# Linear attention and a squared-ReLU feed-forward on one core: batch 0's attention planned with the rest, first loads in order on the SyncE queue

## The chip, the core and the metric

The kernel runs on one core of one Trainium2 chip. The metric is the device time in microseconds (us) of one execution; the kernel before takes 279.13 us (median of 3 runs, 278.8 to 279.6). A profile of one execution comes with it: its span, from the first to the last instruction, is 276.6 us, and that execution took 278.33 us. Names used: PE (TensorE, matmuls), PEld (the loading of PE's weights), DVE (VectorE), ACT (ScalarE), POOL (GpSimd), SP (SyncE, which only issues transfers here). Each engine runs its own instructions in the order in which they were issued, and waits on semaphores for the others.

## What is computed

```python
def phi(x, c, s):                       # c, s: cosine and sine of the position
    r = np.maximum(x, 0.0)
    return np.concatenate([r * c, r * s], axis=-1)
q_p, k_p = phi(q, cos_w, sin_w), phi(k, cos_w, sin_w)      # (8, 8, 576, 128)
kv  = np.einsum('bhsf,bhsd->bhfd', k_p, v)
z   = np.sum(k_p, axis=2)
num = np.einsum('bhsf,bhfd->bhsd', q_p, kv)
den = np.einsum('bhsf,bhf->bhs', q_p, z)[..., None] + 1e-06
x   = (num / den).transpose(0, 2, 1, 3).reshape(4608, 512)
h   = np.maximum(x @ w_in, 0.0)                            # w_in 512 x 2048
out = (h * h) @ w_out                                      # w_out 2048 x 512
```

q, k and v are 8 batches x 8 heads x 576 positions x 64, in float32. There is no softmax: per head a 128 x 64 matrix kv and a vector z are summed over the positions, and every position is then one small product with them. The feed-forward network takes the 4608 rows of x.

## The kernel before, in words

**Tiling.** A batch's 576 positions are four row blocks j = 0 to 3 of 128 positions ("main") and a tail of 64. For each block the cosine and sine features of k and q are made by `relu_scale` (lines 405 and 407, tiles kp and qp), v is cast to bf16 with a column of ones (vx, `copy`, line 412), and PE sums kv and z over the blocks (65 columns per head, tile kvz). q's features are transposed, multiplied by kvz (numerator and denominator), divided on DVE (den, x), and x is transposed to xT. Batch 0 and batch 1 transpose on PE (lines 580 and 668); later batches by transfers (lines 567 and 656). The feed-forward part works on halves of a batch's main rows (256 columns): weights `w1sb` (w_in in bf16, four pieces of 512 columns of w_in, so pieces 0 to 3 hold the blocks 0 to 3, 4 to 7, 8 to 11 and 12 to 15 of 128) times xT, relu on ACT (tile rt or rs), square on DVE (gT), then `w2sb`. Batches 3 to 7 use a Strassen-like scheme of seven products with sums of weights (w1s, made on DVE from w1sb early on) in place of eight; all but batch 0 use it for the second product.

**What sets the order.** From batch 0's third row block on, the order of every engine is the result of `Planner.plan` (line 127 on): a list scheduler with a cost per operation and engine, a place ("slot") for each PE operation from its position, a due time for the others, and pools of buffers. Operations that may run on ACT or DVE are put on one by it. `SHIFTS` is a list of corrections "operation number : shift of its place or due time : engine". Operations of the pseudo-engine GIVEN stand for things that are already under way at a known time, such as the first loads. PE takes the candidate that can start earliest by the planner's times. The order is written into the program, and the semaphores see to the dependences.

**The prologue** (lines 1057 to 1136), the order of which is written by hand: k of batch 0 is issued on SP; kt (k's tail), v, vt, q in two parts, the four w1 pieces, qt and the first w2 piece follow one after another on POOL. 31 matmuls on zeros (line 1069) keep PE busy until k and v have come. Then k's features (cosine on DVE, sine on ACT), v's casts, 40 matmuls into the two banks of kv, the features, transposes and numerators of row blocks 0 and 1 for all 8 heads, a divide per block, seven more matmuls without result (line 1132) and the transposes of x. The planner's clocks start after it (line 1219: PE at 16.8, ACT at 17.3, DVE at 17.1).

**The start of the planned part.** Features of q for row blocks 2 and 3 and the tail, their transposes and numerators, among the feed-forward groups of batch 0 (`declare_plain`, lines 694 to 724). A group is 8 matmuls: 2 blocks of w1 x 4 parts of the contraction, on 256 columns of xT. The groups of the first piece on the first half (`split`) are cut into two of 128 columns, so that they can begin with row block 0 alone. Planning rates of PE are on line 437: 0.1092 us per 256 columns, 0.0586 per 128, 0.0296 per 65, 0.066 per transpose.

```python
    given = lambda keys, t, **kw: add(("GIVEN", 0.0), lambda _: None, w=keys, pos=t, **kw)
    for i in range(4):
        given([("w1", i)], 12.2, size=2.6)
```

**After that** come, on POOL's queue, q, k and v of batches 1 and 2 and the w2 pieces; from batch 3 on the loads are on SP's queue.

## Time and profile before

| engine | busy us | share of the span |
|---|---|---|
| PE | 269.0 | 97% |
| PEld | 227.8 | 82% |
| DVE | 219.1 | 79% |
| ACT | 192.6 | 70% |
| POOL | 28.4 | 10% |

HBM is read for 36.70 MB and written for 9.44 MB, 167 GB/s over the span; the granted clock of PE is at 0.9 or more of full speed in all 40 slices.

How to read it. A row of the timeline gives the start in us, the duration, the engine (POOL's and SP's transfer issues are rows too), the line, the operation, out<-in with shapes, and in brackets the idle time of that engine just before it with what ended it. In a row of several instructions ("x24") the first start and the total time stand. The busy time of PE also counts matmuls that give no result, such as the first 31 (9.76 us from 1.20 us on). A matmul's own row can miss a few records, weight loads (PEld) have one row for every matmul, so counts go by them. In the rows of busy time by stretch, the columns are the stretch, its length, busy time and number of instructions of PE, PEld, DVE, ACT and POOL, the granted clock, the busy share of the transfer engines, and GB/s. For a tile, "to landing" is the time from the start of an issue until the data are there.

### The profile page before, as it was taken

The numbers are of one execution on the slowest core, as the hardware profiler recorded it, in microseconds if no ns is written. First come the engines' busy times: TensorE is split into PE (matmuls) and PEld (weight loads), VectorE is DVE, ScalarE is ACT, GpSimd is POOL, SyncE is SP. The second block draws the span as 40 slices with busy tenths as digits, with TensorE's granted clock in tenths as the row PEclk, the third lists the DMA queues.
The fourth block names the chain that finished last, engine by engine and source line by source line (L and its number), as shares of the span: only waits on it lengthen the run. The fifth ranks groups of instructions, "written<-read, shape, count | busy, mean of one in ns | idle before, by whom it ended". The sixth has DMA issues, their size and how long they took to land.

```text
span 276.6 us, 7125 instructions
## 1 busy us (share of the span) xinstructions
PE 269.0 (97%) x2846; PEld 227.8 (82%) x2851; DVE 219.1 (79%) x515; ACT 192.6 (70%) x385; POOL 28.4 (10%) x46
## 2 busy tenths in 40 slices
PE   8979999999999999999999999999999999999994
PEld 3658856789888988888888888988988888888883
DVE  1849996998795896799977999799946997279741
ACT  3767862798798796499848995699738643685421
POOL 8925244100000000000000000000000000000000
PEclk9999999999999999999999999999999999999999
DMA  7999999776999999899899428997583301200024
GB/s 228 311 206 287 330 256 374 220 174 148 368 191 257 281 248 238 220 331 160 237 266 377 114 40 167 330 219 210 57 233 77 94 32 42 112 1 2 8 88 134
DMA packets 77824, 53.01 MB, mean 192 GB/s; under 512 B 52032, under 2 KB 73024, under 8 KB 77792
## 3 DMA queue, kind: packets, MB, share of 16 engines
q1 hardware_dynamic: 70368, 37.63, 54.7%
q0 software_dynamic: 7280, 14.81, 19.8%
q8 instruction: 22, 0.36, 0.5%
q10 hardware_dynamic: 144, 0.13, 0.1%
q14 instruction: 10, 0.08, 0.1%
HBM read 36.70 MB, written 9.44 MB: 167 GB/s over the span
## 4 chain that ended last, share of the span: by engine, by line
PE 81%; DVE 11%; DMA 2%; issue 2%; POOL 2%; ACT 1%; POOLq 0%; DVEq 0%
PE banks L429 78%; DVE gT L418 3%; DVE rs L421 3%; DVE gs L426 3%; DMA q<-in_q_dram 2%; PE banks L580 1%; DVE gTt L418 1%; PE banks L668 1%; PE banks L1132 1%; ACT qp L405 1%; POOL kt L365 1%; DVE x L628 1%; POOL vt L365 0%; ACT sums L412 0%; DVE kp L407 0%
## 5 line engine op out<-in xcount | busy, mean ns | idle before, releaser
L429 PEld LDWEIGHTS <-w1sb 128*128 128x128 bf16 x784 | 72.7, 98 | 8.7
L429 PE MATMUL banks<-xT,w1sb 128*128 128x256 bf16 (+1 forms) x576 | 68.3, 267 | 0.1
L429 PEld LDWEIGHTS <-gs 128*128 128x128 bf16 x512 | 49.5, 98 | 7.0 <-DVE gs L426 0.7
L429 PE MATMUL banks<-w2sb,gT 128*128 128x256 bf16 (+1 forms) x284 | 44.8, 295 | 0.2 <-issue 0.2
L429 PEld LDWEIGHTS <-gT 128*128 128x128 bf16 x400 | 37.4, 98 | 7.5
L415 ACT ACTIVATE rt<-banks 128x512 bf16<-128x512 f32 x64 | 37.2, 602 | 9.2 <-PE banks L429 4.5
L429 PEld LDWEIGHTS <-w1s 128*128 128x128 bf16 x320 | 30.6, 98 | 3.9 <-issue 0.2
L429 PE MATMUL banks<-w2sb,gs 128*128 128x256 bf16 x256 | 32.7, 273 | 0.1
L429 PE MATMUL banks<-w2s,gs 128*128 128x256 bf16 x256 | 32.1, 273 | 0.1
L421 DVE CUSTOM_DVE_ANT_0 rs<-banks,sums 128x512 bf16<-128x512 f32 x40 | 27.0, 684 | 3.8 <-ACT sums L829 3.1
L418 DVE TENSOR_TENSOR gT<-rs 128x1024 bf16<-128x1024 bf16 (+1 forms) x50 | 28.0, 580 | 1.2 <-ACT rs L415 0.6
L426 DVE TENSOR_TENSOR ysb<-banks,sums 128x256 f32<-128x256 f32 x32 | 13.5, 422 | 17.6 <-PE banks L429 9.4
L418 DVE TENSOR_TENSOR gT<-rt 128x512 bf16<-128x512 bf16 x48 | 19.4, 420 | 7.1 <-ACT rt L415 7.0
L415 ACT ACTIVATE rs<-banks 128x512 bf16<-128x512 f32 x40 | 23.5, 606 | 2.0 <-PE banks L429 1.8
L405 ACT ACTIVATE kp<-k,sin_col 128x512 bf16<-128x512 f32 x32 | 22.4, 725 | 0.5 <-DMA k<-in_k_dram 0.5
L429 PE MATMUL banks<-xT,w1s 128*128 128x256 bf16 x160 | 22.7, 273 | 0.0
L429 PE MATMUL banks<-xs,w1s 128*128 128x256 bf16 x160 | 22.7, 273 | 0.0
L405 ACT ACTIVATE qp<-q,sin_col 128x512 bf16<-128x512 f32 x32 | 22.0, 720 | 1.0 <-DMA q<-in_q_dram 1.0
L426 DVE TENSOR_TENSOR gs<-gT 128x1024 bf16<-128x1024 bf16 x28 | 19.2, 689 | 3.1 <-PE banks L429 2.7
L628 DVE TENSOR_TENSOR x<-banks,den 128x512 bf16<-128x512 f32 x30 | 20.7, 691 | 1.0
L429 PE MATMUL banks<-xTt,w1sb 128*128 128x256 bf16 x128 | 16.1, 273 | 0.0
L407 DVE TENSOR_SCALAR kp<-k,cos_col 128x512 bf16<-128x512 f32 x26 | 12.0, 501 | 5.0 <-DMA k<-in_k_dram 5.0
(105 smaller groups left out, 362.8 us busy)
## 6 DMA issues: line engine op xcount, KB each, us to landing
out_dram<-ysb SPq DMA_DIRECT2D x13, 512.0 KB, 3.6
k<-in_k_dram SPq DMA_DIRECT2D x6, 1024.0 KB, 6.4
v<-in_v_dram SPq DMA_DIRECT2D x5, 1024.0 KB, 7.5
q<-in_q_dram SPq DMA_DIRECT2D x5, 1024.0 KB, 9.3
v<-in_v_dram POOLq DMA_DIRECT2D x3, 1024.0 KB, 8.2
w1sb<-in_moe_w_in_dram POOLq DMA_DIRECT2D x4, 512.0 KB, 10.9
w2sb<-in_moe_w_out_dram POOLq DMA_DIRECT2D x4, 512.0 KB, 12.4
q<-in_q_dram POOLq DMA_DIRECT2D x2, 1024.0 KB, 9.1
```

What stands on the lines that cost most here:

```text
L365: eng.dma_start(out=tail[g * TAIL : (g + 1) * TAIL, :, :], in_=src[b, g * HH : (g + 1) * HH, MAIN:S, :].rearrange("h p d -> p h d"),)
L405: nc.scalar.activation(out=dst, in_=src, func=ACTF.Relu, scale=col)
L407: nc.vector.tensor_scalar(out=dst, in0=src, scalar1=0.0, scalar2=col, op0=ALU.max, op1=ALU.mult)
L415: nc.scalar.activation(out=out, in_=in_, func=ACTF.Relu)
L418: nc.vector.tensor_tensor(out=out, in0=in_, in1=in_, op=ALU.mult)
L421: nc.vector._custom_dve(TENSOR_ADD_SAT, out=out, in0=in0, in1=in1, s0=float("inf"), s1=0.0)
L426: nc.vector.tensor_tensor(out=out, in0=in0, in1=in1, op=op)
L429: nc.tensor.matmul(out=out, lhsT=lhsT, rhs=rhs, start=start, stop=stop, skip_group_check=True)
L580: nc.tensor.transpose(t[:, h, :], qp_at(b, j)[:, h, :], ident[:, :])
L628: nc.vector.tensor_tensor(out=x_at(b, j).rearrange("p (b k) (l d) -> p b k l d", b=n, l=2), in0=n4[:, :, :, 0:D].rearrange("p b (k l) d -> ...
L668: nc.tensor.transpose(t[:, kb, :], x_at(b, j)[:, kb, :], ident[:, :])
L1132: nc.tensor.matmul(out=banks[:, 6 + i % 2, :], lhsT=ident[:, :], rhs=zeros, start=True, stop=True)
```

## The change

It does five things:

- The hand-written prologue for batch 0's attention is gone. `declare_first` declares the same operations to the planner: features, casts, sums, transposes, numerators, divides of row blocks 0 and 1. Features may run on ACT or DVE, as the planner decides. The planner's clocks start at 8.0 (PE) and 6.3 (ACT, DVE).
- The sums kv, the numerators, the divides and the transposes of x for these two blocks go in halves of the heads, g = 0 and 1, so that half of the heads can go on when half of v has come.
- The first loads are all issued on SP, in the order k, kt, row blocks 0 and 1 of q, vt, v of heads 0 to 3, v of heads 4 to 7, row blocks 2 and 3 of q, qt. POOL issues the four w1 pieces, after an element copy that waits for v of heads 0 to 3.
- The two features of k's row block 3 are made on POOL.
- `fill` puts matmuls on zeros into a spare bank: 28 at the start, and some in the planner's gaps on PE before 16.0 (two and two). The seven of line 1132 and the one of line 1101 are gone. `SHIFTS` and some planning costs are new.

It is for an earlier start of the feed-forward part. The core of the diff:

```diff
 SHIFTS = """
-21:4.5 31:1.0 44:-3.0 53:1.5 60:1.0 74:3.0 80:2.0 93:-7.5 105:-0.5 132:-2.5 134:2.0 146:-7.0
...
+10:-3.5 13:-0.5:DVE 15:0.0:ACT 16:-16.0:DVE 26:14.5 33:-0.5 44:0.0:DVE 50:10.5:DVE 56:0.5:ACT
...
-                o.done = pipe + self.margin
+                o.done = pipe + (self.margin if e != "GIVEN" else 0.0)
...
-    T1, T2, t = {}, {}, 16.8
+    T1, T2, t = {}, {}, 16.4
...
-        load_main(k, "k", 0, 0, nc.sync)
-        load_tail(k, "k", 0, 0, nc.gpsimd)
-        load_main(v, "v", 0, 0, nc.gpsimd)
-        load_tail(v, "v", 0, 0, nc.gpsimd)
         constants()
-        load_main(q, "q", 0, 0, nc.gpsimd, 2)
...
+        for src, nm, part in (
+            (k, "k", 0), (k, "kt", 0), (q, "q", 0), (v, "vt", 0), (v, "v", 0), (v, "v", 1), (q, "q", 1), (q, "qt", 0)
+        ):
...
+        fill(28)
+        for c, col in ((0, cos_col), (D, sin_col)):
+            nc.gpsimd.tensor_scalar(
+                out=at(kp_of(0, J - 1))[:, :, c : c + D], in0=piece("k", 0, J - 1),
+                scalar1=0.0, scalar2=col[:, J - 1 : J], op0=ALU.max, op1=ALU.mult,
+            )
+        nc.gpsimd.tensor_copy(out=w1sb[0:1, 0, 0:1], in_=mem["v"][0:1, 0, 0, 0, 0:1])
         for i in range(4):
             load_w1(i, 4)
-        load_tail(q, "q", 0, 0, nc.gpsimd)
...
+    for keys, t in (
+        ([L("k")], 6.2), ([L("kt")], 6.6), ([(L("q"), 0)], 8.2), ([L("vt")], 8.6), ([(L("v"), 0)], 10.2),
+        ([(L("v"), 1)], 11.9), ([(L("q"), 1)], 13.6), ([L("qt")], 14.0),
+    ):
+        given(keys, t, lat=0.0)
     for i in range(4):
-        given([("w1", i)], 12.2, size=2.6)
+        given([("w1", i)], 11.7, size=2.6)
-    given([loaded["q", 0]], 14.2, lat=0.0)
...
-    t0 = {"PE": 16.8, "ACT": 17.3, "DVE": 17.1, "SP": 10.0, "POOL": 20.0, "GIVEN": 0.0}
+    t0 = {"PE": 8.0, "ACT": 6.3, "DVE": 6.3, "SP": 10.0, "POOL": 14.2, "GIVEN": 0.0}
     with tc.manual_schedule():
         prologue()
+        end = None
         for op in plan.plan(t0):
+            if op.eng == "PE" and op.start < SPARE_UNTIL:
+                if end:
+                    fill(int((op.start - end - 0.2) / 0.22))
+                end = op.end
             op.fn(op.eng)
```

In the order of the changed program, as built, PE runs the 28 matmuls on zeros, 16 transposes of q's features (blocks 0 and 1), the sums kv of heads 0 to 3, numerators of heads 0 to 3, sums of heads 4 to 7, transposes of x of heads 0 to 3, transposes of q's features of blocks 2 and 3, numerators of heads 4 to 7 and of block 2, transposes of x of heads 4 to 7, numerators of block 3, and then the first feed-forward groups. The operations of the planner are numbered in the order of their declaration: 0 to 7 are the GIVEN entries of the eight loads, 8 to 11 those of the w1 pieces 0 to 3.

## The prediction

> **What bounds the kernel now.** I read the busy shares first, then busy time by stretch, then the timeline of the first 26 us, then the weight loads of the feed-forward part (tile w1sb) and the DMA rate in slices of 1 us.

> Section 1 of the page, then the answer on busy time by stretch:

> ```profile
> PE 269.0 (97%) x2846; PEld 227.8 (82%) x2851; DVE 219.1 (79%) x515; ACT 192.6 (70%) x385; POOL 28.4 (10%) x46
> ...
> 8.00:18.03 10.03, 8.30 (x101) 5.12 (x101) 7.74 (x20) 6.16 (x12) 5.43 (x7) 1.00 1.14 259
> 18.03:25.00 6.97, 6.97 (x102) 6.60 (x103) 4.04 (x12) 5.52 (x9) 4.20 (x6) 1.00 1.23 216
> 25.00:61.50 36.50, 36.16 (x375) 26.61 (x378) 33.97 (x95) 24.93 (x46) 11.61 (x17) 1.00 1.00 284
> 61.50:270.00 208.50, 208.18 (x2235) 184.88 (x2233) 170.37 (x382) 151.52 (x313) 0.56 (x1) 1.00 0.68 171
> ```

> The first column after the stretch is its length, the second PE's busy time. From 18.03 us on PE has no gap worth naming (0.34 us in 25 to 61.5, 0.32 us in 61.5 to 270). So PE bounds the kernel, and the span is PE's work plus what it loses before it is saturated. Much of its busy time before that is warm-up matmuls on zeros.

> The timeline around the moment of saturation, and GpSimd's two waits for w1 pieces:

> ```profile
> 17.25 1.33 ACT L405 ACTIVATE qp<-q,sin_col 128x512 bf16<-128x512 f32 x2
> 18.03 0.45 PEld L580 LDWEIGHTS <-qp 128*128 128x128 bf16 x8 [1.47 <-ACT qp L405]
> 18.43 1.38 PEld L429 LDWEIGHTS <-w1sb 128*128 128x128 bf16 x24
> 19.77 0.49 PEld L580 LDWEIGHTS <-qp 128*128 128x128 bf16 x8
> ...
> 21.71 0.90 POOL L357 DMA_DIRECT2D v<-in_v_dram  x1 [0.29 <-DMA w1sb<-in_moe_w_in_dram]
> 24.24 1.25 POOL L365 DMA_DIRECT2D kt<-in_k_dram  x2 [1.63 <-DMA w1sb<-in_moe_w_in_dram]
> ```

> The last real gap is 1.3 to 1.5 us, for ACT's sine feature of q, ending at 18.03. The w1 loads themselves (tile w1sb), and the DMA rate in 40 slices of 1 us from 0:

> ```profile
> L372 POOL DMA_DIRECT2D w1sb<-in_moe_w_in_dram x4: 747/829/925, 8.0 to 10.4; - x4
> DMA to landing us min/median/max: 8.1/10.9/13.6
> ...
> GB/s 0 9 157 323 384 406 340 377 393 315 303 345 211 196 203 207 216 199 206 205 209 207 263 212 214 344 419 410 397 401 291 220 230 376 411 388 214 225 209 218
> ```

> Landings: the first piece at 8.0 + 8.1 = 16.1; the third at 21.7 (GpSimd's v load reuses its semaphore and waited until then); the fourth at 24.2. The median is the mean of the middle two, issued at 8.8 and 9.6, so the second landed at 2 x 10.9 + 18.4 - 21.7 = 18.5. The rate says why they are so late: slices 0 to 11 add to 3.35 MB, and batch 0's q, k, v with tails are 3.41 MB. So the engines are filled by attention inputs until 12 us and by w1 after that, at some 207 GB/s: 0.524 MB in 2.53 us a piece.

> [...]SyncE's k and GpSimd's v share 323 to 406 GB/s.[...] The same-shaped cosine features of k at 6.3 us take 468 to 791 ns[...].[...] here the granted clock is 1.00 in every stretch above[...].

> **The change part by part.**

> The measure. PE runs in order and does the same result matmuls before and after (only warm-up matmuls differ, 39 against 32). So I compare at a moment when PE is saturated from there on: time minus result work done so far, the deficit. Rates from starts of weight loads in the timeline: 128 columns 1.34/24 = 0.056 us (18.43 to 19.77), a transpose 0.40/8 = 0.05, 65 columns 0.27/8 = 0.034 (22.88 to 23.15), 256 columns 1.67/16 = 0.104 (20.94 to 22.61). Before, by 18.03: 56 matmuls of 65 columns and 24 transposes, 1.90 + 1.20 = 3.10 us. Deficit 14.93 us. The change is worth what it takes off this.

> 1. All first loads on SyncE, in the order k, kt, half of q, vt, half of v's heads, other half, rest of q, qt. No bytes are saved; qt (0.131 MB) moves from behind w1 to ahead of it, 0.131/0.38 = 0.35 us of transfer, up to 0.6 at the slices' 210 GB/s[...]. GpSimd's issues (0.7 to 0.9 us each) vanish, so the iotas come 3.6 us earlier and the sine tables no longer gate: k's landing does, some 6.2 us as before.

> 2. w1 is issued once the first half of v has landed. By bytes k, kt, half q, vt, half v are 2.36 MB, which the slices above reach at 9.0 us; plus the 1.3 us from the end of bytes to landing that w1's first piece shows (12.2 + 2.53 to 16.1), 10.3. Four issues of 0.83 us end at 13.7. Transfers of w1 start at about 12, when some 0.3 MB of the rest is left. The engines are full either way, so the third piece lands at 21.7 + 0.35 = 22.05 (21.3 to 22.5).

> 3. Two key features on GpSimd. No row here shows such an operation. VectorE takes 0.47 us[...].[...]

> 4. The attention of the first two row blocks in halves of heads. VectorE carries it. 28 warm-up matmuls end at 10.3 (31 ended at 10.96, the late ones 0.21 us apart). First query transpose to 10.6, copy 0.41 (11.0), v cast 0.6 (11.6), copy 0.41 (12.0), two casts (13.2), first divide 0.17 + 0.20 + 0.69 and issue (14.3), two cosine features 0.47 each (15.25), half kvz copy 0.4 (15.65), 1024-wide copy 0.69 (16.35), two half divides 0.16 + 0.18 + 0.42 each (17.9). Two transposes and eight numerators later the first w1 matmul starts, at 18.2. ACT's part (features 0.72, copies 0.58) runs beside and ends sooner. By then PE has done 16 more transposes and 16 more numerators than before at 18.03: 72 x 0.034 + 40 x 0.05 = 4.45 us. Deficit 13.75: 1.2 us gained. The first w1 piece (16.4) is no bound.

> 5. The order after it, which decides. In the built kernel PE's first 32 w1 matmuls wait for the first w1 load; the next group waits for the **third**, and the second load is awaited only after that. VectorE's sums confirm which is which: the first w1s sum reads blocks 8 and 9, piece 2 counted from 0, and waits on the same semaphore. The planner orders the four equal-time entries by due time, and SHIFTS moves entry 10, piece 2, by -3.5. But the loads are issued 0, 1, 2, 3. Behind this wait on PE stand all later matmuls, and ACT and DVE wait for those. PE reaches it at 18.2 + 32 x 0.056 + 4 x 0.05 = 20.2, and piece 2 lands at 22.05: a new wait of 1.85 us. Work done by then: 4.45 + 1.79 + 0.20 = 6.44. Deficit 22.05 - 6.44 = 15.6, against 14.93: **0.7 us worse**.

> 6. From there on. Piece 1 is long there, piece 3 (24.6) is needed at 15.6 + 11.0 = 26.6. q of batch 1 now goes before the first w2 piece: 24.6 + 2.6 + 2.6 = 29.8 (2.6 from GpSimd's waits), needed at 15.6 + 18.3 = 33.9. Later w2 pieces keep 3 us or more. The redrawn SHIFTS and costs reorder the rest; PE has at most 0.7 us of gaps there to win, and could lose more. I take 0. The tail is the same four steps.

> Sum: 279.13 + 0.7 = 279.8 us.

> **Rivals.** (a) Piece 2 is there in time: if SyncE's queue fills the engines from 1.5 us (slices 1 and 2 hold 166 KB where 700 would fit) and piece 2 lands by 20.3, the 1.2 us of step 4 stay: 277.9. Against it: k alone had SyncE's queue to itself in those slices before, too. Between: a landing at 21.0 gives 279.13 - 0.4 = 278.8. (b) [...]features of 2 us on GpSimd, holds VectorE back 2 us or more: first w1 matmul at 20.3, and piece 2 is no longer the bound: deficit 15.9 at least, 280.1 to 280.8; a late w1 issue adds as much. For it: the 791 ns above. (c) The new order stalls PE later on, by 1 us in sum over VectorE-bound stretches: 280.8.

> **How the numbers follow.** The forecast, piece 2 as the bound at 21.5 to 22.5 and the time at 279.3 to 280.3, gets 0.55; (a) with its in-between 0.2; (b) 0.13; (c) 0.12. The time is the forecast's, 279.8. The range 278.4 to 281.2 leaves out most of (a) at the low end and the worst of (b) and (c). 0.3% is 0.84 us: faster than 278.29 needs piece 2 before 20.6, 0.17; slower than 279.97 is (b), (c) and a third of the forecast, 0.41; within, 0.42.

> **What would show it.** PE waiting some 1.8 us on DMA w1sb near 20 to 22 us, w1 landings near 16.4, 19, 22 and 24.6, first w1 matmul near 18.2, the sum of PE's gaps after 25 us under 1 us. Wrong if no wait for w1sb appears, if PE reaches the first w1 matmul after 20 us, or if GpSimd's features take over 2 us.

## The result and the profile after

The changed kernel takes 282.38 us (median of 4 executions, 281.22 to 283.42) against 279.37 us for the kernel before beside it: a ratio of 1.0103 (95% interval 1.0054 to 1.0152), 3.0 us slower. Medians are over all executions of a run; the ratios leave out executions more than 1.5% above the fastest of their kernel. Four more executions on another chip gave 282.34 us, 1.0095 (1.0058 to 1.0132). The forecast was 279.8 us with a range to 281.2. Its mechanism, the wait for the third w1 piece, is there; the time lies 1.2 us above the range's end.

Engine shares of the changed kernel (section 1 of its page), then busy time by stretch; the columns are as before.

```profile
PE 269.7 (96%) x2839; PEld 228.5 (81%) x2844; DVE 222.5 (79%) x520; ACT 191.9 (68%) x384; POOL 27.1 (10%) x40
```

```profile
8.00:18.19 10.19, 8.76 (x125) 5.96 (x125) 9.01 (x25) 7.59 (x16) 9.10 (x10) 1.00 1.07 243
18.19:28.00 9.81, 7.04 (x74) 5.87 (x71) 6.20 (x17) 2.87 (x6) 3.71 (x6) 0.83 1.18 259
28.00:61.50 33.50, 33.06 (x340) 24.14 (x342) 29.36 (x77) 21.59 (x40) 11.71 (x16) 1.00 0.98 279
61.50:270.00 208.50, 207.46 (x2235) 184.28 (x2234) 173.22 (x393) 154.56 (x314) 0.00 (x0) 1.00 0.70 171
```

The busy shares of the whole run moved by two points at most. The second row is where the two kernels part: PE is busy for 7.04 of 9.81 us, where the kernel before had no gap worth naming, and its granted clock averages 0.83. In the last row PE's gaps are 1.04 us, against 0.32 before.

PE's weight loads around the new wait:

```profile
18.19 1.80 PEld L430 LDWEIGHTS <-w1sb 128*128 128x128 bf16 x32
19.95 0.27 PEld L674 LDWEIGHTS <-x 128*128 128x128 bf16 x4
23.16 0.84 PEld L430 LDWEIGHTS <-w1sb 128*128 128x128 bf16 x8 [2.94 <-DMA w1sb<-in_moe_w_in_dram]
24.05 0.58 PEld L674 LDWEIGHTS <-x 128*128 128x128 bf16 x4
```

The first w1 matmul comes at 18.19 us, as worked out (18.2). Then 32 matmuls, four transposes, and 2.94 us without a weight load until the third w1 load has landed. The four transposes at 19.95 took 0.27 us; the four at 24.05, after the gap, took 0.58. That is the clock, at 0.50 from 23.80 us on. Mean granted clock in two stretches of 4 us (the last three columns are the clock, the transfer engines' share and GB/s):

```profile
20.00:24.00 4.00, 1.23 (x14) 0.97 (x12) 1.32 (x5) 0.60 (x1) 1.36 (x2) 0.97 1.24 207
24.00:28.00 4.00, 4.00 (x26) 3.09 (x24) 3.14 (x9) 1.32 (x3) 0.93 (x2) 0.60 1.11 337
```

From 24 to 28 us PE is busy all the time at 0.60 of its speed (0.50 from 23.80 to 27.21). What leads to the late piece, from the chain of work that ended at the wait (start, duration, what):

```profile
6.40 4.61 POOL kp L1081 x2
11.02 0.33 POOL w1sb L1085
11.34 0.30 issue
11.64 1.85 POOL w1sb L373 x2
13.49 9.62 DMA w1sb<-in_moe_w_in_dram
```

and the loads' landing (tile w1sb), then the transfer rate in 40 slices of 1 us:

```profile
L373 POOL DMA_DIRECT2D w1sb<-in_moe_w_in_dram x4: 747/817/1002, 11.6 to 14.2; - x4
...
DMA to landing us min/median/max: 5.8/8.8/11.5
```

```profile
GB/s 0 16 172 317 386 325 346 311 359 371 364 348 199 46 139 198 213 197 208 204 207 207 206 207 313 434 395 206 193 295 398 414 287 217 200 364 424 386 225 209
```

The w1 issues begin at 11.64 us, not near 10.4, and the third piece lands at 13.49 + 9.62 = 23.11, not 22.05. In the slices from 12 to 15 us the transfer engines carry 199, 46 and 139 GB/s: the last bytes of the attention inputs and the first of w1 both fall into the slice from 13 to 14. Before, w1 followed without such a hole.

The last part lies far behind. PE's waits in 100 to 130 us:

```profile
PE banks L430 <- DMA qpT<-qp: 1.0, 2, 0.7
```

These are query transposes of batch 4, made by transfers on SyncE's queue. The kernel before has no wait for them in its profile. It issues both transposes of row blocks ahead of that of the tail:

```profile
104.02 6.71 SPq L567 DMA_TRANSPOSE qpT<-qp  x2
110.89 1.19 SPq L567 DMA_TRANSPOSE qpTt<-qpt  x1
```

The prediction's measure, time less useful PE work, gives the account of the profiled executions (a count of weight loads from timeline rows drifts by up to five, 0.4 us at the end; I take 0.0555 us per transpose and the planning rates of line 437, so the 14.93 of the prediction becomes 15.04). At the end of the wait the deficit is 16.71 against 15.04: **1.7 us**. From there to 34.55 us it grows to 18.27, where the kernel before goes from 15.04 to 15.27 by 31.77: **1.3 us**, the clock. The last product's weight load comes at 275.45 against 271.47, 3.98 later, so **about 1.0 us** is lost after that, most of it between 107 and 128 us. The tail behind it is the same. The two profiled executions lie 4.0 us apart (278.33 and 282.30 us), the medians 3.0: the profile of the kernel before is of one of its faster executions, so the three parts divide 4.0 us and not 3.0.

### The profile page after: what moved, and what is told of

It is laid out like the page before. It is cut to its first block, busy times and chain, and to the rows that moved or that the text cites. A ratio compares the mean times of both kernels' runs of the same rounds, so it can differ in the third digit from the quotient of the medians.

```text
span 280.5 us, 7121 instructions
## 1 busy us (share of the span) xinstructions
PE 269.7 (96%) x2839; PEld 228.5 (81%) x2844; DVE 222.5 (79%) x520; ACT 191.9 (68%) x384; POOL 27.1 (10%) x40
## 4 chain that ended last, share of the span: by engine, by line
PE 86%; DMA 7%; POOL 2%; ACT 2%; issue 1%; SPq 0%; POOLq 0%
PE banks L430 85%; DMA w1sb<-in_moe_w_in_dram 3%; DMA qpT<-qp 2%; DMA k<-in_k_dram 2%; POOL kp L1081 2%; POOL w1sb L373 1%; ACT rt L416 1%; ACT qp L406 1%; PE banks L586 1%; PE banks L674 1%; ACT kvz L413 0%; ACT ysb L952 0%; SPq L573 0%; ACT ysb L961 0%; POOL w1sb L1085 0%
## 5 line engine op out<-in xcount | busy, mean ns | idle before, releaser
L430 PEld LDWEIGHTS <-w1sb 128*128 128x128 bf16 x784 | 73.6, 99 | 12.0 <-DMA w1sb<-in_moe_w_in_dram 2.9
L430 PE MATMUL banks<-xT,w1sb 128*128 128x256 bf16 (+1 forms) x576 | 69.8, 270 | 2.8 <-DMA w1sb<-in_moe_w_in_dram 2.8
L416 ACT ACTIVATE rt<-banks 128x512 bf16<-128x512 f32 x64 | 37.7, 600 | 14.5 <-PE banks L430 10.6
L430 PEld LDWEIGHTS <-gT 128*128 128x128 bf16 x400 | 38.0, 98 | 8.5
L430 PE MATMUL banks<-w2sb,gT 128*128 128x256 bf16 (+1 forms) x284 | 44.2, 295 | 0.2
L406 ACT ACTIVATE qp<-q,sin_col 128x512 bf16<-128x512 f32 x30 | 21.0, 724 | 1.1 <-DMA q<-in_q_dram 1.1
L406 ACT ACTIVATE kp<-k,sin_col 128x512 bf16<-128x512 f32 x29 | 20.2, 723 | 0.0
L836 ACT COPY sums<-banks 128x512 f32<-128x512 f32 x20 | 11.8, 588 | 7.0 <-PE banks L430 6.6
## 6 DMA issues: line engine op xcount, KB each, us to landing
k<-in_k_dram POOLq DMA_DIRECT2D x2, 1024.0 KB, 12.6
```

What stands on the lines that cost most here:

```text
L406: nc.scalar.activation(out=dst, in_=src, func=ACTF.Relu, scale=col)
L416: nc.scalar.activation(out=out, in_=in_, func=ACTF.Relu)
L430: nc.tensor.matmul(out=out, lhsT=lhsT, rhs=rhs, start=start, stop=stop, skip_group_check=True)
L836: add(("ACT", 0.5), lambda _: nc.scalar.copy(out=at(u2), in_=bank(Bk)), r=[Bk], w=[u2])
```

## The experiments

The theory at first: the order of the w1 loads against their use makes the wait, GpSimd's long features make it longer, the wait halves the clock, and the new order on SyncE's queue makes the query transposes late. The rival: the loss is the volume of transfers, or lies in the new order elsewhere. "Clock" below is the mean granted clock of an execution; a half-clock stretch of 3.41 us (23.80 to 27.21 in the changed kernel) takes it from 0.997 or more to 0.994 or less. None of the 178 executions of the kernel before that ran beside the experiments is below 0.997.

### The w1 loads in the order of their use

```diff
-        for i in range(4):
+        for i in (0, 2, 1, 3):
             load_w1(i, 4)
```

> The changed kernel with the four w1 loads issued in the order 0, 2, 1, 3, which is the order in which the program uses the pieces; nothing else differs. Theory A (TensorE's wait of 2.8 us is the mismatch between issue order and order of use, and the half clock after it follows from the wait): piece 2 lands second, near 20.8 us, TensorE reaches it near 20.4, so the wait is 0.4 us or less, and piece 1, third, near 23.1, is awaited 0.4 us or less; the granted clock is 1.00 in every slice; the deficit (time less useful TensorE work) behind these waits is 14.7 to 14.9 us in place of 18.3. Time 279.1 us (278.6 to 279.8), 3.3 us less than the changed kernel. Rival B (the loss is the volume of transfers or lies in the later order of the new plan, whatever the w1 order): 281.9 us or more.

Measured: 278.56 us (277.04 to 279.74, 20 executions), ratio 0.9977 (0.9960 to 0.9995). One edit takes away 3.5 us by the ratios, 3.8 by the medians, and the kernel is slightly faster than the one before. PE's weight loads in this run:

```profile
18.36 1.80 PEld L430 LDWEIGHTS <-w1sb 128*128 128x128 bf16 x32
20.12 0.27 PEld L674 LDWEIGHTS <-x 128*128 128x128 bf16 x4
20.34 0.81 PEld L430 LDWEIGHTS <-w1sb 128*128 128x128 bf16 x8
21.16 0.32 PEld L674 LDWEIGHTS <-x 128*128 128x128 bf16 x4
21.44 0.81 PEld L430 LDWEIGHTS <-w1sb 128*128 128x128 bf16 x8
23.52 5.57 PEld L430 LDWEIGHTS <-w1sb 128*128 128x128 bf16 x52 [1.27 <-DMA w1sb<-in_moe_w_in_dram]
```

Piece 2, now issued second, needs no wait; piece 1, now issued third, still comes at 23.5 us and is awaited for 1.27 us, more than the 0.4 expected, so the deficit is 15.1 and not 14.8. The clock stayed full in 19 of 20 executions. The rival falls.

### The wait filled, not shortened

12 matmuls on zeros (512 columns) go to bank 7 directly ahead of the group that waits:

```diff
...
+            if getattr(op, "piece", 0) == 2 and not warmed:
+                warmed = True
+                fill(12, 7)
```

> The changed kernel with 12 extra matmuls on zeros of 512 columns, about 2.6 us of TensorE work without result, put directly ahead of the group that waits for the third w1 piece. The landing of that piece stays near 23.1 us, so the wait is filled, not shortened. Theory A (the half clock in 24 to 27 us comes from the idle time of 2.8 us and costs 1.3 to 1.6 us): granted clock 1.00 in all slices, time 280.9 us (280.6 to 281.3). Rival B (the clock drop is something else, or costs nothing since other engines bound that stretch): 282.4 us, and the clock still at 0.50 in 24 to 27 us.

Measured: 280.48 us (20 executions), all at a clock of 0.997 or more, ratio 1.0055 (1.0037 to 1.0073). That is 1.9 us below the changed kernel by the medians, 1.3 by the ratios. Repeated on another chip (further down) it took 281.19, 1.2 below by the medians; but its ratio of 1.0092 is only 0.1 to 0.3 us below the changed kernel's two (1.0095 and 1.0103), and these ran on other chips. The same stretches:

```profile
20.00:24.00 4.00, 3.95 (x37) 2.34 (x35) 1.46 (x4) 1.19 (x2) 1.41 (x3) 1.00 1.24 206
24.00:28.00 4.00, 3.74 (x37) 3.37 (x37) 3.71 (x11) 1.79 (x3) 1.54 (x2) 1.00 1.11 334
```

So the half clock follows from the idle wait: filled, it is gone in 28 of 28 executions of the two runs. What that is worth is less sure: 0.1 to 1.9 us by these comparisons, 1.3 in the profiled execution above. The rest of what the load order costs is the wait. With 5 such matmuls, which leave part of the wait idle:

> The changed kernel with 5 matmuls on zeros in place of 12 ahead of the group that waits for the third w1 piece, about 1.1 us of the wait of 2.8 filled and 1.7 to 1.9 us left idle. If a single gap near 3 us is what halves the clock (theory A): no execution below 0.997, median 280.5 us, as with 12. If the share of activity decides (theory B): a part of the executions, fewer than half, still at 0.995 or below and 1.5 us longer.

Measured: 282.17 us (279.55 to 283.45, 4 executions), all four at a full clock; PE waited 1.6 us in the profile. The clock answers as theory A has it, the time does not: in that profile a wait of 0.9 us for a copy on ACT and 0.8 us for query transposes come on top. At full clock these executions are no faster than the changed kernel at half clock (282.38), so they do not confirm the price; four executions do not say more.

The changed kernel again:

> The changed kernel once more, unaltered, for many executions with the mean granted clock of each. Theory A (the half clock behind the long wait comes in a part of the executions, and costs about 1.7 us where it comes): two groups, near 282.4 us at a mean clock of 0.993 to 0.994 and near 280.7 us at 0.998 to 1.000, the first with at least half of the executions. Rival B (the clock is not what separates the executions): no such grouping, median 282.4 us at any clock.

Measured: 282.34 us, and all four executions at 0.991 to 0.994, as the four of the first measurement. The two groups did not show in it, since all eight fell to half clock. They show in the exchange of transposes below, which has the same w1 wait: 11 of 16 executions at 0.994 or less, median 281.60, and 5 at 0.999 or more, median 279.93. **1.7 us** apart. Those that fell may also have waited longer, so this need not be the clock alone.

### GpSimd's features shorter, then moved

First, the features for one head of eight only (a memset, not shown, sets the rest to zero; the other seven heads of k's row block 3 are left out):

```diff
...
-                out=at(kp_of(0, J - 1))[:, :, c : c + D], in0=piece("k", 0, J - 1),
+                out=at(kp_of(0, J - 1))[:, 0:1, c : c + D], in0=piece("k", 0, J - 1)[:, 0:1],
```

> The changed kernel with GpSimd's two features of k's row block 3 made for one head of eight only; it leaves out the other seven heads of that row block (their features are zero). Theory A (GpSimd's long features, 2.48 and 2.14 us, hold back the issue of w1 and with it the landing of the third piece): w1 issue begins near 10.5 us in place of 11.64, third piece lands near 22.0, TensorE waits 1.7 us; time 281.2 us if the clock still drops to half after that wait, 279.9 us if it does not. Rival B (the 16 transfer engines are full, so an earlier issue lands nothing earlier): third piece at 23.1, 282.4 us.

Measured: 281.43 us (4 executions; three at a clock of 0.998 or more, 281.2 to 281.5, one at 0.994, 283.6). GpSimd in this run:

```profile
6.26 0.93 POOL L1082 TENSOR_SCALAR kp<-k,cos_col 128x64 bf16<-128x64 f32 x1 [3.49 <-DMA k<-in_k_dram]
7.02 0.67 POOL L1082 TENSOR_SCALAR kp<-k,sin_col 128x64 bf16<-128x64 f32 x1
11.37 0.44 POOL L1086 CAST w1sb<-v 1x1 bf16<-1x1 f32 x1 [3.68 <-DMA v<-in_v_dram]
12.11 3.34 POOL L373 DMA_DIRECT2D w1sb<-in_moe_w_in_dram  x4 [0.31 <-POOL w1sb L1086]
```

This part of my theory falls. GpSimd is free at 7.7 us and then stands for 3.68 us, until v's first half lands; w1 is issued later than in the changed kernel. In the chain above the features ended at 11.0 us, 0.3 after v had landed, and the trace named them. v's first half was there at 10.7 us in the changed kernel's profile (VectorE's cast of it starts at 10.73) and at 11.2 to 11.9 in the three that show a wait for it among the first four experiments (the wait filled by 12, the shorter features, the transposes exchanged). From the first w1 issue to PE's resuming is 11.52 us in the changed kernel and 11.49 to 11.73 in these four: the transfers take the same time, only their start moves.

Second, the features on VectorE, with the new w1 order, and beside them two operations of the same form on constants, on GpSimd before 6.5 us (not shown, nor is the w1 order):

```diff
...
-            nc.gpsimd.tensor_scalar(
+            nc.vector.tensor_scalar(
                 out=at(kp_of(0, J - 1))[:, :, c : c + D], in0=piece("k", 0, J - 1),
```

> The changed kernel with the w1 loads in the order 0, 2, 1, 3, and with the two features of k's row block 3 on VectorE ahead of all others in place of GpSimd. Beside that GpSimd makes two operations of the same form on constants before 6 us, overwritten later, to time them while VectorE is idle. Theory A (GpSimd needs over 2 us for such an operation by itself, but did not set the time, because w1 waits for v's first half anyway, which lands at 10.7 to 11.9): the two early operations take 2.0 to 2.5 us each; w1 issue again at 11.4 to 12.6 us; time within 0.4 us of the run that has the new w1 order alone, 278.6 us. Rival B (the slow features were the delay, by themselves or by holding VectorE up): w1 issue at 11.0 or earlier, 277.6 us. Rival C (GpSimd is slow only against a busy VectorE)[...].

Measured: 278.53 us (9 executions), 0.997 (0.9948 to 0.9992), the same as with the w1 order alone (278.56). GpSimd in this run:

```profile
2.45 3.98 POOL L1082 TENSOR_SCALAR kp<-sums 128x512 bf16<-128x512 f32 x2
11.29 0.43 POOL L1092 CAST w1sb<-v 1x1 bf16<-1x1 f32 x1 [4.87 <-DMA v<-in_v_dram]
```

Two in 3.98 us: 1.99 us each with VectorE idle, against 0.48 us for such a feature on VectorE with GpSimd making none (last section). The operation is slow by itself, and hidden all the same.

### The query transposes exchanged

Batch 4's transpose of row blocks 2 and 3 goes ahead of that of the tail on SyncE's queue, which is the order of the kernel before:

```diff
+        order = plan.plan(t0)
+        i, j = (order.index(turned["q", 4, n]) for n in (J // 2, 1))
...
+        order[i], order[j] = order[j], order[i]
```

> The changed kernel with two transposing transfers of batch 4's query features exchanged on SyncE's queue: the one of row blocks 2 and 3 goes ahead of that of the tail. Theory A (the last third of the loss is TensorE's waits for these transposes near 116 and 121 us, the second of which is 0.95 us): the second wait falls to 0.2 us or less; time 281.6 us, 0.7 to 0.9 less than the changed kernel. Rival B (the wait is bounded by its inputs or comes back further on): no change, 282.4 us.

The changed kernel's timeline around these transposes, first SyncE's issues, then PE's weight loads:

```profile
111.13 3.00 SPq L573 DMA_TRANSPOSE qpT<-qp  x1
114.30 1.24 SPq L573 DMA_TRANSPOSE qpTt<-qpt  x1
115.59 2.05 SPq L573 DMA_TRANSPOSE qpT<-qp  x1
```

```profile
116.36 0.30 PEld L430 LDWEIGHTS <-qpT 128*128 128x128 bf16 x8 [0.58 <-DMA qpT<-qp]
...
121.54 0.30 PEld L430 LDWEIGHTS <-qpT 128*128 128x128 bf16 x8 [0.95 <-DMA qpT<-qp]
```

Measured: 281.41 us (279.56 to 283.82, 16 executions). Both waits are gone from its profile (of an execution at full clock, in which PE comes to them 1.9 us earlier), and the deficit goes from 18.09 at 114 us to 18.23 at 127, where the changed kernel's went from 19.27 to 20.74. Among executions at half clock the median is 281.60 (11) against 282.38 (8): 0.8 us, as expected, but in a spread of 3 us. Hence a pair on one chip with the long wait filled, so that the clock is out of it:

> The changed kernel with the 12 matmuls on zeros ahead of the group that waits for the third w1 piece, and with the exchange of the two query transposes of batch 4. Theory A (the waits for those transposes cost 0.7 us wherever TensorE comes late): 0.5 to 0.8 us less than the run beside it, about 279.8 us. Rival B (the waits come and go with each execution's transfers and the exchange moves them elsewhere): within 0.3 us of the run beside it, 280.5 us.

> The changed kernel with the 12 matmuls on zeros, unaltered, as the measure for the run beside it: 280.5 us (279.9 to 281.0), every execution at a mean clock of 0.997 or more.

Measured: 280.21 us (279.83 to 282.28, 9 executions) with the exchange and 281.19 us (280.18 to 282.66, 8) without; ratios to the kernel before 1.0078 (1.0045 to 1.0111) and 1.0092 (1.0060 to 1.0123). The profiles agree with theory A: no wait for these transposes in the first, 0.9 us in the second. The medians do too, by 1.0 us, the ratios by 0.4; the intervals overlap. And where the early waits are short:

> The run with the w1 order and VectorE's features (278.5 us, without its two timing operations on GpSimd), and the exchange of the two query transposes on SyncE's queue; w1 is held back by v's first half, as in the changed kernel. Theory A (the late query transposes cost 0.6 to 0.8 us also where the early waits are short): 277.8 us (277.4 to 278.2), no execution with a mean clock of 0.994 or below, since TensorE has no gap over 1.3 us. Rival B (with earlier work ahead of it the exchange has nothing to remove, or delays the tail's transpose by as much): 278.5 us.

(w1 order and VectorE's features, with the exchange.) Measured: 278.62 us (277.19 to 279.91, 21 executions), 0.9992 (0.9975 to 1.0009), nothing won over 278.5: rival B. The profiles without the exchange fit that: each of the six with the late w1 piece shows this wait (0.6 to 1.4 us), the two with the w1 order mended and w1 behind v do not. A ninth, in the next part, shows the longest: w1 is early there, but the clock fell near 19 us, and PE comes to the first of these transposes at 114.6 us, where the two without a wait come at 112.5 and 112.9. So the third part of the loss goes with PE's being late, and is not a cost of the new order by itself. What links the two I did not find, and the exchange is no sure cure: of seven profiles with it five show no such wait, one 0.4 us, and one (the run with fillers below) 1.8 us for the transposes of queries and their tail.

### w1 issued earlier

With the w1 order and VectorE's features (without the two timed operations on GpSimd), the element copy that holds w1 back reads q's first half in place of v's:

```diff
-        nc.gpsimd.tensor_copy(out=w1sb[0:1, 0, 0:1], in_=mem["v"][0:1, 0, 0, 0, 0:1])
+        nc.gpsimd.tensor_copy(out=w1sb[0:1, 0, 0:1], in_=mem["q"][0:1, 0, 0, 0, 0:1])
```

> As the run before, with one edit more: the element copy that holds the w1 loads back reads the first half of q (lands near 8.3 us) in place of v's first half (10.7 to 11.9). Theory A (the third piece lands late because the issue is late: the transfer engines run dry between 12 and 15 us): w1 issue at 8.8 to 9.2 us, no slice between 11 and 16 us under 180 GB/s, third piece at 21.2 (20.6 to 21.8), TensorE's waits for w1 0.4 us or less, 277.6 us. Rival B (w1 then takes the rate from v's second half and q's second half, and the first w1 matmul comes 1 us or more later): 278.5 us or more.

Measured: 279.26 us (276.53 to 283.38, 20 executions). The w1 issue began at 9.10 us, the hole in the rate and PE's waits for w1 are gone, as theory A has it, but 8 executions are at 0.994 or less, with a median of 282.15; the other 12 have 277.93. Its profile is of one of the eight (283.31 us, clock 0.988). The clock falls in it twice: at 19.05 us, after gaps of PE of 1.1 us and less, and at 121.44, after a wait for the query transposes, which stand in the unexchanged order here:

```profile
120.98 0.42 PE L430 MATMUL banks<-kvz,qpT 128*128 128x65 bf16 x8 [1.87 <-DMA qpT<-qp]
```

From 114 to 127 us this execution loses 4.0 us by the deficit, the changed kernel 1.5. With the exchange of transposes as well, twice:

> As the run before, with the exchange of the two query transposes of batch 4 on SyncE's queue as well. Theory A (the two losses are apart, and add): 0.6 to 0.8 us below the run before, 276.9 us, below both the changed kernel and the one before it. Rival B (with the early part mended the transposes are no longer late, or another wait takes their place): same as the run before, 277.6 us.

> The run with all four edits once more, unaltered, for more executions. Theory A (the earlier w1 issue is worth 0.5 to 1.0 us over the run beside this one, since the w1 waits of 0.7 and 0.7 us go and the first w1 matmul comes 0.5 us later): 277.0 to 277.6 us in the executions at full clock. Rival B (the earlier issue gives back as much as it wins): 277.8 us or more in those.

Measured: 277.61 us (4 executions), then 279.64 us (21; 276.94 to 282.54), ratios 0.9921 and 0.9997 (0.9971 to 1.0024). The first was luck: 1 of 4 and 8 of 21 executions are at half clock for a stretch. At full clock the median of both is 277.6. ScalarE in the second:

```profile
18.86 0.51 ACT L406 ACTIVATE qpt<-qt,sin_col 128x256 bf16<-128x256 f32 x1 [2.43 <-DMA qt<-in_q_dram]
19.27 0.99 ACT L413 COPY sums<-banks 128x1024 bf16<-128x1024 bf16 x1
```

q's tail, the last on SyncE's queue, now shares the rate with w1 and lands near 18.8 us. ScalarE waits 2.43 us for it, and behind it stands the copy that PE's last transpose of x waits for; the first w1 matmul comes at 20.64 us. PE's gap before that transpose is 2.27 us, and the clock does not fall in this profile. Two attempts on this. First, nine more matmuls on zeros in PE's gaps, four ahead of the first sums kv and five ahead of the last two transposes of x:

```diff
+                    fill(4 if (j, g) == (0, 0) else 0)
...
+                    fill(g * (2 + j), 7)
```

> As the run with all edits (w1 order, features on VectorE, w1 behind q's first half, query transposes exchanged), and with nine more matmuls on zeros in gaps of TensorE before its saturation: four ahead of the first sums kv (gap of 1.07 us), two and three ahead of the last two transposes of x (gaps of 0.4 and 1.1 us). Theory A (the clock falls on a low share of activity over some microseconds, not on one long gap: in the two runs before this one it fell near 19 us, in 8 of 20 and 1 of 4 executions, after a stretch of short gaps): no execution below a mean clock of 0.997, median 277.5 us (277.0 to 278.0), all executions under 280 us. Rival B (the falls of the clock have nothing to do with the gaps): a fifth or more of the executions at 0.994 or below, those near 281 to 282 us.

Measured: 278.11 us (276.77 to 283.87, 22 executions), 0.9966 (0.9942 to 0.9990); 4 of 22 still at 0.994 or less. Fewer than 9 of 25, but not none: neither theory as written. That the falls came near 19 us is seen in one profile only, and where they came in the other executions is not known. Second, q's tail loaded ahead of q's second half:

```diff
-            (v, "v", 1), (q, "q", 1), (q, "qt", 0)
+            (v, "v", 1), (q, "qt", 0), (q, "q", 1)
```

> As the run with all four edits, with one more: q's tail is loaded ahead of q's second half instead of behind it. Theory A (w1's early transfers take the rate from q's tail; ScalarE's sine feature of the tail waits for it, and behind it stands the copy that TensorE's last transposes of x wait for): the tail's sine feature starts by 16.0 us in place of 17.3 to 18.9, first w1 matmul at 18.2 to 18.6 us in place of 19.1 to 20.6, at most one execution in ten at a mean clock of 0.994 or below, median 277.3 us (276.8 to 277.8). Rival B (q's second half, later by the tail's bytes, becomes the wait in its place, or the falls of the clock have another cause): 278.5 us or more, a fifth or more of the executions at 0.994 or below.

Measured: 277.64 us (276.78 to 284.49, 11 executions), 0.9946 (0.9913 to 0.9978). ScalarE's row:

```profile
15.85 0.51 ACT L406 ACTIVATE qpt<-qt,sin_col 128x256 bf16<-128x256 f32 x1
```

The wait for the tail is gone, the first w1 matmul comes at 18.37, and the six executions at full clock lie at 276.8 to 277.6. But 5 of 11 fell to half clock (279.8 to 284.5), so the late tail was a wait, and the falls do not need it. Of 56 executions with the early w1 issue and no fillers, 22 fell; of 50 with the new w1 order and w1 behind v, one. Why so many more fell was not settled: only one of the 22 is profiled. What the traces show of the clock stands in the last section. Median times in this group were won and lost by it, so I name the w1 order alone (or with the features on VectorE) as the version to keep: 278.5 us, clearly below the changed kernel and 0.2 to 0.3% below the kernel before. That gain is small and not certain, since with the exchange added the interval takes in 1.

## Why the prediction was wrong

**Step 5, the order, was right in kind.** PE waits where it was said to, for the piece that was said, at 20.4 us. Exchanging two load issues removes most of it and 3.5 to 3.8 us with it.

**Steps 1 and 2 failed in a size.** "The engines are full either way, so the third piece lands at 21.7 + 0.35": they were not full. v's first half landed at 10.7 to 11.9 and not at 10.3, element copy and issue took 0.66 us more, the w1 issue began at 11.64 (up to 12.64 in other profiles), and the rate fell to 46 GB/s in between. The third piece follows the first issue by 11.5 to 11.7 us in five profiles; 10.4 + 11.65 would have been 22.05. The term was the start of the issue, 1.1 to 1.2 us too early, and the wait 2.8 us instead of 1.85. Two readings beside it were loose and changed nothing: k and v share the rate in one slice only (SyncE's queue alone carries the slices from 3 to 5 us), and 3.41 MB are batch 0's q, k and v without q's tail, 3.54 with it.

**The clock was left out.** The prediction read a granted clock of 1.00 in every stretch of the kernel before. It did not ask what the gap that it forecast would do to it. Here the clock fell in all eight executions of the changed kernel, with gaps of 2.8 and 2.9 us in the two that are profiled. In other profiles it fell after 1.87 us and after gaps of 1.1 us and less (both w1 behind q's first half) and did not after 2.27 (w1 behind q's first half, transposes exchanged), 2.70 (transposes exchanged alone) and 2.98 (features for one head). Whether a wait of 1.85 us, as forecast, would have lowered the clock is therefore open. What is known is the price in the profiled execution: 1.3 us, which the prediction put at nothing.

**Step 3 had no measured time for the features on GpSimd, and it cost nothing.** They took 2.48 and 2.14 us. The prediction named "over 2 us" as what would refute it; two runs show that it does not matter, since v's landing holds w1 back as long. VectorE's four k features end at 8.4 us, and its lost time, 0.4 us on a k feature and 0.7 on two of q, did not delay the first w1 matmul.

**Step 4 was right**, in its chain too: the first w1 matmul at 18.19 us against 18.2, deficit 13.7 against 13.75, and VectorE's last half divide (from 17.37, for 0.42 us) ends at 17.8 against 17.9.

**Step 6, "I take 0", missed about 1 us** of waits for query transposes. Two runs with the transposes exchanged are without the wait in the profile; how much time that is worth, 0.8 to 1.0 us by medians, is not fixed beyond doubt, and with the early wait mended it is nothing.

**The rivals.** (a), all of step 4's gain kept at 277.9, is about what the w1 order and the early issue give in executions at full clock. (b) and (c) named the late issue and the later stall with 1 us each; the prediction took them as alternatives, while both came on top of the forecast.

## What to carry to other kernels

Compare the order in which loads are issued with the order in which the built program first uses each piece; one exchange was worth more here than the whole rewrite around it. When a forecast contains a new idle stretch of PE, price what it may do to the clock behind it too: here the clock fell to 0.50 after stretches of 1.87, 2.8 and 2.9 us, and once after several of 1.1 us and less, and stayed full after others of 2.27 to 2.98. And where the trace names the engine that ended a wait last, look how close the second releaser stood: removing GpSimd's 4.6 us of features changed nothing, since a load landed at nearly the same moment.

## What the runs showed of the hardware

```profile
20.38:23.80 3.42, 0.65 (x7) 0.59 (x7) 0.74 (x3) 0.42 (x1) 1.16 (x2) 1.00 1.24 207
23.80:27.21 3.41, 3.41 (x20) 2.57 (x19) 2.61 (x8) 1.16 (x2) 1.13 (x2) 0.50 1.09 358
```

```profile
15.63:19.05 3.42, 1.85 (x35) 1.53 (x33) 3.09 (x11) 2.07 (x5) 2.86 (x4) 1.00 1.24 204
19.05:22.46 3.41, 3.41 (x38) 3.41 (x38) 2.00 (x7) 1.10 (x3) 1.72 (x3) 0.50 1.24 207
118.03:121.44 3.41, 1.54 (x25) 0.97 (x24) 1.00 (x5) 1.12 (x3) 0.00 (x0) 1.00 0.73 152
121.44:124.86 3.42, 3.42 (x24) 2.48 (x23) 2.06 (x5) 1.36 (x3) 0.00 (x0) 0.50 1.08 381
```

With GpSimd's features shortened, PE's gap was 2.98 us, but one of the points (the first rise, at 5.61, plus 5 times 3.413, so 22.67) divides it, and the clock stayed full:

```profile
19.26:22.67 3.41, 1.60 (x29) 1.42 (x26) 1.60 (x6) 1.19 (x2) 1.58 (x3) 1.00 1.24 206
22.67:26.09 3.42, 2.25 (x23) 2.05 (x24) 2.27 (x7) 0.67 (x2) 0.90 (x1) 1.00 1.19 286
```

So this gap of 2.98 us, divided by a point, left the clock full, while the changed kernel's of 2.8 us, almost all of it between two points, was followed by 3.41 us at 0.50. That is read from the traces afterwards, and no run tests it; nor do the traces say sharply how much work in a stretch goes with a full clock behind it. The four falls inside the 17 profiles follow stretches in which PE was busy for 0.65 us (changed kernel), 0.63 (its second profile), 1.54 and 1.85 (w1 behind q's first half, the 1.85 mostly with transposes and matmuls of 65 columns); after 1.60 us, in the run with GpSimd's features shortened, the clock stayed. Why 8 of 8, 11 of 16 and 1 of 4 executions with nearly the same gap fell was not shown.

A max-and-multiply of 128 x 512 elements from float32 to bf16 takes GpSimd 1.99 us with VectorE idle, and 2.48 and 2.14 beside VectorE's features; 128 x 64 take 0.67 and 0.93. VectorE beside it, in the changed kernel:

```profile
6.32 0.49 DVE L408 TENSOR_SCALAR kp<-k,cos_col 128x512 bf16<-128x512 f32 x1 [4.96 <-DMA k<-in_k_dram]
6.72 0.91 DVE L408 TENSOR_SCALAR kp<-k,sin_col 128x512 bf16<-128x512 f32 x1
7.55 0.47 DVE L408 TENSOR_SCALAR kp<-k,cos_col 128x512 bf16<-128x512 f32 x1
7.95 0.47 DVE L408 TENSOR_SCALAR kp<-k,sin_col 128x512 bf16<-128x512 f32 x1
8.35 1.64 DVE L408 TENSOR_SCALAR qp<-q,sin_col 128x512 bf16<-128x512 f32 x2
```

GpSimd's first feature runs from 6.40 to 8.88. Of the three VectorE features that start and end within that span one takes 0.91 us and two take 0.47: VectorE finishes three instructions, two of them unslowed, during one of GpSimd's. The two slow each other all the same: in the run with w1 behind q's first half, where GpSimd makes no features, VectorE's k features take 0.48 to 0.49 us each and the two of q 0.88, against 0.91 (one of four) and 1.64 here, and GpSimd's two take 0.6 us more together than with VectorE idle.
